# First token list from six half batches instead of eight, and the late half batches' logits in one matmul group each

## The chip, the cores and the metric

The kernel runs on one core of one Trainium2 chip. Its time is the device time of that core in microseconds, from launch to end. A profiled execution of the same program gives the trace that is read below. In it PE is the matrix engine, DVE the vector engine, ACT the scalar engine, POOL GpSimd and SP the engine that issues most DMAs; L56 is the line of a helper through which nearly all PE, DVE and ACT instructions pass, so groups are told apart by the names of their tiles.

## The reference, cut to what matters

A causal 7-tap filter per head runs along each sequence (8 sequences of 3584 tokens, 192 features, 8 heads of 24), with softmaxed taps; its output is routed over 8 experts with a capacity of 3584 tokens each, highest logits first, and every token passes the two-layer ReLU network of its expert.

```python
x_unf = x_pad[:, idx, :].reshape(B, S, K, H, group)
out = np.einsum('hk,bskhg->bshg', w, x_unf)          # w = softmax(weight) over the 7 taps
...
logits = x @ w_gate                                  # x: (28672, 192), w_gate: (192, 8)
order = np.argsort(-logits.flatten())
for idx in order:
    tok, e = (int(idx) // E, int(idx) % E)
    if assigned[tok] >= 0 or counts[e] >= cap:
        continue
    assigned[tok] = e
    counts[e] += 1
...
for e in range(E):
    mask = assigned == e
    h = np.maximum(x[mask] @ w1[e], 0.0)             # 192 -> 1024
    out[mask] = h @ w2[e]                            # 1024 -> 192
```

## The kernel before, in words

**Filter stage.** The tokens come in 16 half batches of 1792. `conv` (L196) loads one as 118 rows by 16 windows by 192 features, multiplies it for each of the 8 heads with a banded 118x128 matrix (PE `cv<-X,TH`, two records in the trace for one matmul), copies the sums out on ACT (`a<-cv`) and stores them to `attn` in DRAM. `transp` (L208) turns the result in 32x32 blocks on DVE (`aT<-a`, four per half batch). `logits` (L217) multiplies it with the gate weights: 24 matmuls for a half batch (six chunks of features, four column tiles of 32 columns, `pl<-aT,c_mu`), and `end` (L1560) transposes the sums (`pt<-ident,L`) into the table `LT` and takes each token's largest logit (`top`, L317). `LT` is 128 partitions by 8 experts by 256 columns; a half batch fills 16 columns. `gate(i, u)` (L1573) issues a third of the 24 matmuls. Since the conv matmuls of the next half batches run in between, `mid(h)` (L1603), called after the matmul of head h, puts the four transposes of half batch i-1 and, between them, the three gate groups and the end of half batch i-2 into the list `left`, and pops one entry (two, once the first list is done). From half batch LAG = 13 on, it pops nothing until the first list is done (`got`).

**Routing in the background.** The routing is one chain of Python generators, `Steps` (L75), with the parts `half(0)`, `tail`, `half(1)` and `rest`. While the program is written, `hook` runs a step of it when three modelled clocks (PE, DVE, ACT, class `Meter`) say that its inputs will be there and that DVE is not too far ahead; a step may ask to wait (`yield PEW`, a time, or `"cols", n` for n columns of `LT`). All of this is settled at build time; on the chip each engine executes its instructions in the order written, and waits on semaphores only.

A threshold `Ts` is found first (`thresh`, L322; its last part wants 96 columns). Tokens whose largest logit reaches it are settled at once on their best expert. A list of them is built from a set of columns of `LT` in these steps: `settle` marks them in `F`; `count` sums them per column (`bg<-ones,F`); `place` gives each its slot (`bg<-F,U`, `bg<-U,tot`, `bg<-ones,tot` for an offset of earlier columns); `slots` splits the slot numbers; `sort` brings the columns into slot order with one matmul per column (`bg<-X,oa`, 16 wide) from one-hot tiles `oa` made on DVE, and `turn` transposes the result on PE (`bg<-identb,X`); `sort4` does the same with 32-column tiles (`bg<-oa,X`), and turns it by a trip through DRAM on SP's queue (`otab<-X`, then `X<-otab`); `columns` makes the one-hot `c_oh`; `gather` adds up the list in PSUM (`bg<-iq,ones`, then 16 matmuls `bg<-c_oh,X`); `tokens` turns it into row numbers (`ia`, `ja`) on DVE. After `sort4`, `gather` is held back in the model by `there`, 10 us after the last copy.

- `half(0)`: threshold, then columns 0 to 127 (eight half batches), with `sort` and `turn`. It gives the first 512 tokens of each expert.
- `tail`: logits of half batches 14 and 15, which run in the first expert tile.
- `half(1)`: columns 128 to 255, with `sort4`, and `counts` and `open` ahead of its gather. It gives up to 2048 tokens of each expert.
- `rest`: seven rounds that settle the other tokens (`rounds`, L743), a last choice (`final`, L863), and a list of 1536 tokens per expert by two `sort4` and two `gather`, then `tokens` into `ib`, `jb`.

**Expert stage.** `FFN.run` (L1424) goes over 56 tiles of 512 tokens: tiles 0 to 7 are the first 512 tokens of the experts, tiles 8 to 31 the next 1536, tiles 32 to 55 the rest. For each tile and each of f = 0 to 7 it writes the first layer's five matmuls of chunk f (`ph`), then eight matmuls of the second layer of the tile before (`y`), with background steps at four points. Numbers are kept in two parts (`hh`, `hl`), hence the DVE work on each chunk. Rows of `attn` are gathered two tiles ahead on POOL (`xg<-attn,ja`). Ahead of that, at f = 0 of tile i, the row numbers of tile i+2 are asked for, and what of the background is then missing is written out at once:

```python
if t < 4:
    if len(bg.gens) > 1:
        bg.drain(1)
    return [(ja if rows else ia)[:, e, 4 * t + b:4 * t + b + 1] for b in range(4)]
if bg.gens:
    bg.drain()
```

Tiles 8 to 31 pass their inputs through DRAM on SP's queue (`turn` of `FFN`, L1388: `scr<-xs`, then `xs<-scr`), at f = 6, two tiles ahead. If a list is too short or an expert too full, a flag `bad` sends the program through a general path after the end; one of its conditions is that the first list has less than 512 tokens of an expert (`counts`, L657).

Of the kernel before, what the change touches and what calls it, by code (L numbers as in the profile page):

```python
# [259 lines left out]
class Route:  # L260
# [15 lines left out]
    def consts(self):  # L276
# [12 lines left out]
        self.g1 = cst.tile([128, 2], F32, name="g1")  # L289
        for h in range(2):  # L290
            P.tensor_scalar(self.g1[:, h:h + 1], pf, 1.0 + 128 * h, None, op0=OP.add)
# [81 lines left out]
    def settle(self, h):  # L373

        V, wk = self.nc.vector, self.wk
        s = slice(128 * h, 128 * h + 128)
        yield "cols", 128 * h + 128
        if h == 0:
            self.F = wk.tile([128, 8, G], BF, name="F")
        m = wk.tile([128, 128], F32, name="m_f")  # L380
        V.scalar_tensor_tensor(m, self.M1[:, s], self.Ts, self.M1[:, s], op0=OP.is_lt, op1=OP.add)
        for q in range(2):
            e = slice(4 * q, 4 * q + 4)
            V.tensor_tensor(self.F[:, e, s], self.LT[:, e, s], m[:, None, :].to_broadcast([128, 4, 128]),
                            op=OP.is_equal)
            yield PEW if q else None


    def count(self, F, h):
        nc, wk = self.nc, self.wk  # L390
        V, PE = nc.vector, nc.tensor
        s = slice(128 * h, 128 * h + 128)
        if h == 0:
            self.tot = [None, None]
            self.sl = wk.tile([128, G], F32, name="sl")
        ps = self.bg()
        for e in range(8):
            PE.matmul(ps[:, e:e + 1], F[:, e, s], self.ones[:, 0:1], start=True, stop=True, skip_group_check=True)
        t = self.tot[h] = wk.tile([128, 8], BF, name="tot%d" % h)
        nc.scalar.activation(t, ps[:, 0:8], AF.Copy)  # L400
        yield PEA

    def place(self, F, h, base):
# [3 lines left out]
        s = slice(128 * h, 128 * h + 128)  # L407
        SP = wk.tile([128, 8, 128], F32, name="X0")
        for q in range(2):
            ps = self.bg()  # L410
            f = F[:, 4 * q:4 * q + 4, s]
            PE.matmul(ps, self.U, f, start=True, stop=False, skip_group_check=True)
            for u in range(4):
                e = 4 * q + u
                o = ps[:, 128 * u:128 * u + 128]
                b = lambda t: t[:, e:e + 1].to_broadcast([128, 128])
# [1289 lines left out]
```

## Time and profile before

| | us |
|---|---|
| median of 3 runs | 1246.0 |
| lowest and highest run | 1242.64, 1251.04 |
| the profiled execution's own time | 1251.99 |
| span of its trace, first to last instruction | 1250.2 |
| PE busy | 1208.1 |
| DVE busy | 979.4 |
| ACT busy | 547.4 |
| POOL busy | 531.7 |
| DMA | 205.09 MB, 164 GB/s over the span |

The span is read by stages: the filter stage ends with the last `cv` at about 161 us of the trace, and the 56 tiles of the expert stage fill the rest. In the rows, the first column is the start in us from the span's start, the second the time until the end of the merged rows; matmuls overlap, so that what a group costs is read from its start to the start of what follows. `[1.53 <-DMA ...]` is idle time ahead of the row and what ended it.

### The profile page before, as it was taken

What the parts mean: (1) busy time and instruction counts of PE and PEld (TensorE: products, weight loads), DVE (VectorE), ACT (ScalarE), POOL (GpSimd) and SP (SyncE); (2) the same over time, 40 slices, a digit from 0 to 9 for tenths busy, and PEclk for the clock granted to TensorE, in tenths of its full rate; (3) what the DMA queues carried; (4) which work ended last, traced back from release to release, by engine and by line L of the source; (5) the groups of instructions that cost most, each with busy time, mean ns of one, the idle gap of its engine ahead of it and who ended that gap; (6) DMA issues with size and microseconds to landing.
All of it is one profiled execution on the core that took longest, in us unless ns stands there. A gap on an engine that the chain in (4) does not pass through costs nothing.

```text
span 1250.2 us, 21752 instructions
## 1 busy us (share of the span) xinstructions
PE 1208.1 (97%) x7702; PEld 1036.5 (83%) x7702; DVE 979.4 (78%) x2131; ACT 547.4 (44%) x1220; POOL 531.7 (43%) x528
## 2 busy tenths in 40 slices
PE   4999989999999999999999989999999999999997
PEld 2445568889988989889888879999999999999996
DVE  7388669889898898989888865777777777777772
ACT  4454555656444544444543333333443333443331
POOL 3000344535455545555454434445444544444522
PEclk9999999999999999999999999999999999999999
DMA  9999889999725463444344563114133222413100
GB/s 221 339 348 310 294 299 316 280 321 302 270 82 155 128 188 113 158 149 149 123 144 135 178 164 121 36 48 154 67 126 107 95 97 96 157 56 137 49 23 28
DMA packets 125188, 205.09 MB, mean 164 GB/s; under 512 B 21440, under 2 KB 85392, under 8 KB 121360
## 3 DMA queue, kind: packets, MB, share of 16 engines
q1 hardware_dynamic: 82464, 127.22, 31.9%
q0 software_dynamic: 21504, 44.07, 11.7%
q10 hardware_dynamic: 21104, 32.34, 7.8%
q8 instruction: 62, 1.02, 0.3%
q14 instruction: 54, 0.44, 0.1%
HBM read 118.64 MB, written 84.93 MB: 163 GB/s over the span
## 4 chain that ended last, share of the span: by engine, by line
PE 85%; DVE 6%; DMA 5%; issue 1%; SPq 1%; ACT 1%; POOL 1%; ACTq 0%; POOLq 0%; DVEq 0%
PE ph L56 40%; PE y L56 38%; PE bg L56 3%; PE cv L56 3%; DMA X<-in_x_dram 2%; DVE X L56 1%; DVE aT L56 1%; DMA wgr<-in_moe_w_gate_dram 1%; DMA raw<-in_moe_w_dram 1%; DMA X<-otab 1%; PE pl L56 1%; DMA xg<-attn,ja 1%; DVE hl L56 0%; PE px L56 0%; DMA otab<-X 0%
## 5 line engine op out<-in xcount | busy, mean ns | idle before, releaser
L56 PE MATMUL y<-w,hh 128*128 128x384 f32 x1792 | 536.8, 355 | 0.0
L56 ACT ACTIVATE hh<-ph 128x512 fp32r<-128x512 f32 x448 | 267.2, 597 | 486.3 <-PE ph L56 485.2
L56 PE MATMUL y<-w,hl 128*128 128x192 f32 x1792 | 449.7, 251 | 0.0
L56 DVE SCALAR_TENSOR_TENSOR hl<-ph,hh 128x512 fp32r<-128x512 f32 x448 | 308.5, 689 | 138.6 <-ACT hh L56 134.0
L56 PE MATMUL ph<-xa,w 128*128 128x512 f32 x1344 | 395.6, 402 | 0.0
L56 PEld LDWEIGHTS y<-w,hl 128*128 128x128 f32 x1792 | 341.7, 191 | 16.4
L56 PEld LDWEIGHTS y<-w,hh 128*128 128x128 f32 x1792 | 337.1, 188 | 20.4 <-issue 2.2
L56 PEld LDWEIGHTS ph<-xa,w 128*128 128x128 f32 x1344 | 218.9, 189 | 20.2 <-issue 1.0
L1348 POOL DMA_INDIRECT out_dram<-yo,ia x128 | 138.9, 1085 | 225.9 <-DVE yo L56 188.1
L1348 POOL DMA_INDIRECT out_dram<-yo,ib x96 | 95.9, 999 | 220.1 <-DVE yo L56 212.7
L56 PE MATMUL ph<-xd,w 128*128 128x512 f32 x448 | 178.9, 399 | 1.3 <-DVE xd L56 1.3
L56 PE MATMUL ph<-xd,dl 128*128 128x512 f32 x448 | 174.6, 390 | 0.2 <-DVE dl L56 0.2
L56 DVE STREAM_TRANSPOSE xs<-xg 32x128 f32<-32x128 f32 (+2 forms) x408 | 164.8, 404 | 6.6
L1273 POOL DMA_INDIRECT xg<-attn,ja x128 | 139.3, 1088 | 47.6 <-issue 40.4
L56 PE MATMUL cv<-X,TH 118*128 118x384 f32 x256 | 101.5, 523 | 19.5 <-DVE TH L56 12.5
L1273 POOL DMA_INDIRECT xg<-attn,jb x96 | 103.4, 1078 | 29.3 <-issue 29.3
L56 ACT ACTIVATE yt<-y 128x192 f32<-128x192 f32 x224 | 73.1, 326 | 94.3 <-PE y L56 92.3
L56 DVE TENSOR_TENSOR yo<-y,yt 128x192 f32<-128x192 f32 x224 | 79.5, 355 | 41.3 <-ACT yt L56 39.2
L56 PEld LDWEIGHTS ph<-xd,w 128*128 128x128 f32 x448 | 84.3, 188 | 21.4 <-DVE xd L56 1.7
L56 PEld LDWEIGHTS ph<-xd,dl 128*128 128x128 f32 x448 | 84.5, 189 | 19.7 <-issue 0.5
L56 PEld LDWEIGHTS cv<-X,TH 118*128 118x128 f32 x256 | 45.3, 198 | 49.9 <-issue 14.1
L56 ACT ACTIVATE a<-cv 128x384 f32<-128x384 f32 x128 | 59.5, 492 | 50.8 <-PE cv L56 33.0
(238 smaller groups left out, 893.1 us busy)
## 6 DMA issues: line engine op xcount, KB each, us to landing
attn<-a ACTq DMA_DIRECT2D x16, 1344.0 KB
w<-kw SPq DMA_DIRECT2D x14, 1536.0 KB
w<-kv SPq DMA_DIRECT2D x14, 1536.0 KB
kw<-w SPq DMA_DIRECT2D x48, 256.0 KB
kv<-w SPq DMA_DIRECT2D x32, 384.0 KB
X<-in_x_dram SPq DMA_DIRECT2D x17, 672.0 KB
X<-in_x_dram ACTq DMA_DIRECT2D x15, 672.0 KB
scr<-xs SPq DMA_DIRECT2D x96, 96.0 KB
```

Source lines behind the costliest of these rows:

```text
L56: return f(*a, **k)
L1273: self.nc.gpsimd.indirect_dma_start(out=t[:, b], out_offset=None, in_=self.attn[0:rows], in_offset=bass.IndirectOffsetOnAxis(ap=idx[b], ax ...
L1348: st = self.nc.gpsimd.indirect_dma_start(out=self.out, out_offset=bass.IndirectOffsetOnAxis(ap=idx, axis=0), in_=o, in_offset=None, bounds ...
```

## The change

`settle`, `count`, `place`, `columns`, `slots`, `sort`, `turn` and `gather` no longer take a half h of 128 columns but a part (first column, columns), and cut their tiles to its width. The first list is made of part (0, 96), six half batches. What was `half(1)` becomes `second`: columns 96 to 223 go through `sort4` as before; while its turn through DRAM is under way, the last part (224, 32) is settled and counted and the sums of `counts` are taken; then the first of the two is gathered, and the part of 32 columns is placed, sorted with `sort` (32 matmuls), turned on PE and gathered; `tokens` and `open` follow. The final lists of `rest` keep two halves of 128. In `mid`, half batches 11, 12 and 13 (from LAG = 13 on) get their 24 gate matmuls in one group, ahead of the transposes of the half batch behind them.

```diff
+PARTS = ((0, 96), (96, 128), (224, 32))
+HALVES = ((0, 128), (128, 128))
...
-    def place(self, F, h, base):
+    def place(self, F, part, bases):
...
-                if base is not None:
-                    PE.matmul(o, b(self.tot[base]), self.ones, start=False, stop=False, skip_group_check=True)
-                PE.matmul(o, b(self.tot[h]), self.U, start=False, stop=(u == 3), skip_group_check=True)
+                for p in bases:
+                    m = p[1]
+                    PE.matmul(o, self.tot[p][:, e:e + 1].to_broadcast([m, 128]), self.ones[0:m, 0:n],
+                              start=False, stop=False, skip_group_check=True)
+                PE.matmul(o, self.tot[part][:, e:e + 1].to_broadcast([n, 128]), self.U[0:n, 0:n],
+                          start=False, stop=(u == 3), skip_group_check=True)
...
-    def sort(self, h, nt, base, per=8):
+    def sort(self, part, nt, bases, per=8):
...
-        while z < 128:
+        while z < n:
...
-                if z == 64:
-                    yield from self.columns(h, nt, base)
+                if z == n // 64 * 32:
+                    yield from self.columns(part, nt, bases)
...
-    def lists(self, F, nt, h, base, idx, row, *part, between=None, swap=False):
+    def listed(self, F, nt, part, bases, between=None):
+
+        yield from self.place(F, part, bases)
+        yield from self.slots(F, part, between is None)
         if between is None:
-            yield from self.sort(h, nt, base)
-            yield from self.turn()
+            yield from self.sort(part, nt, bases)
+            yield from self.turn(part[1])
         else:
-            yield from self.sort4(h, nt, base)
+            yield from self.sort4(part, nt, bases)
             yield from between
-        yield from self.gather(nt, base is None)
-        yield from self.tokens(nt, idx, row, *part, swap=swap)
+        yield from self.gather(part[1], nt, not bases)
...
-        def half(h):
-            if h == 0:
-                yield from r.thresh(0.905)
-            yield from r.settle(h)
-            yield from r.count(r.F, h)
-            if h:
-                yield from r.counts(NE)
-            yield from r.lists(r.F, TA, h, 0 if h else None, *((ia, ja) if h else (ia0, ja0, 8, 4)),
-                               between=r.open() if h else None, swap=h == 1)
+        def early():
+            yield from r.thresh(0.905)
+            yield from r.settle(PARTS[0])
+            yield from r.count(r.F, PARTS[0])
+            yield from r.listed(r.F, TA, PARTS[0], ())
+            yield from r.tokens(TA, ia0, ja0, 8, 4)
+
+        def second():
+            yield from r.settle(PARTS[1])
+            yield from r.count(r.F, PARTS[1])
+            yield from r.listed(r.F, TA, PARTS[1], PARTS[0:1], between=third())
+            yield from r.listed(r.F, TA, PARTS[2], PARTS[0:2])
+            yield from r.tokens(TA, ia, ja, swap=True)
+            yield from r.open()
+
+        def third():
+            yield from r.settle(PARTS[2])
+            yield from r.count(r.F, PARTS[2])
+            yield from r.counts(NE)
...
-        bg = Steps(nc, r, (half(0), tail(), half(1), rest()))
+        bg = Steps(nc, r, (early(), tail(), second(), rest()))
...
+        def gates(i):
+            for u in range(3):
+                gate(i, u)
...
                 if i and h == 0:
+                    if i >= LAG:
+                        left.append(partial(gates, i - 2))
                     for u in range(4):
                         left.append(partial(k.transp, i - 1, u))
-                        if i > 1:
+                        if 1 < i and (u == 3 or i < LAG):
                             left.append(partial(gate, i - 2, u) if u < 3 else partial(end, i - 2))
```

Three places show how the instructions move. The first is on PE at the end of the filter stage, from the gather of the first list on, up to the end of half batch 12's logits; `cv` is the conv matmul of a head, `pl` the gate matmuls, `pt` the transpose of the sums. Before:

```order
L56 MATMUL cv<-X,TH 128x384 x4
L56 MATMUL pl<-aT,c_mu 32x128 x8
L56 MATMUL cv<-X,TH 128x384
L56 MATMUL pl<-aT,c_mu 32x128 x8
L56 MATMUL cv<-X,TH 128x384
L56 MATMUL pl<-aT,c_mu 32x128 x8
L56 MATMUL cv<-X,TH 128x384
L56 MATMUL pt<-ident,L 128x128
L56 MATMUL cv<-X,TH 128x384
L56 MATMUL pl<-aT,c_mu 32x128 x8
```

After:

```order
L56 MATMUL cv<-X,TH 128x384 x4
L56 MATMUL pl<-aT,c_mu 32x128 x24
L56 MATMUL cv<-X,TH 128x384 x2
L56 MATMUL pt<-ident,L 128x128
L56 MATMUL cv<-X,TH 128x384
L56 MATMUL pl<-aT,c_mu 32x128 x24
L56 MATMUL cv<-X,TH 128x384 x2
L56 MATMUL pt<-ident,L 128x128
```

The three groups of eight, with a conv matmul between them, are one group of 24. The gather ahead of these rows follows head 0 of half batch 14 before and head 2 of half batch 13 after, so the same half batch's logits also stand some heads earlier.

The second is on PE in the expert stage, at the last gather of the last list. `X_...` is a slab of the sort (`bg<-oa,X`) and, under another number, the turned list (`bg<-c_oh,X`); `y` is the second layer, `ph` the first. Before, these rows stand in f = 4 of tile 29, while the sort's last matmul stands in f = 7 of tile 28:

```order
L56 MATMUL y<-w_7888,hh 128x384
L56 MATMUL y<-w_7888,hl 128x192
L56 MATMUL y<-w_7888,hh 128x384
L56 MATMUL y<-w_7888,hl 128x192
L56 MATMUL ph<-xa,w_8385 128x512 x3
L56 LDWEIGHTS ones
L56 MATMUL bg<-iq,ones 128x192
L56 LDWEIGHTS X_9383
L56 MATMUL bg<-c_oh,X_9383 128x24
```

After, from the sort's last matmul on, in f = 7 of tile 29 and f = 0 of tile 30:

```order
L56 MATMUL bg<-oa,X_9233 32x128
L56 MATMUL y<-w_7978,hh 128x384
L56 MATMUL y<-w_7978,hl 128x192
L56 MATMUL y<-w_7978,hh 128x384
L56 MATMUL y<-w_7978,hl 128x192
L56 MATMUL y<-w_7978,hh 128x384
L56 MATMUL y<-w_7978,hl 128x192
L56 MATMUL y<-w_7978,hh 128x384
L56 MATMUL y<-w_7978,hl 128x192
L56 LDWEIGHTS ones
L56 MATMUL bg<-iq,ones 128x192
L56 LDWEIGHTS X_9699
```

The whole background has moved back by one tile by then, and the row numbers for tile 32 are asked for at f = 0 of tile 30, so the rest is written out there: eight `y` matmuls stand between the sort's last matmul and the gather, where before there were those eight, four whole steps of both layers and three `ph`.

The third is SP's queue at the same place; `scr` is the DRAM buffer of the tiles' inputs, `otab` that of the list, `kw` and `kd` are kept weights. Before:

```order
L546 DMA otab_81<-X_9012 128x2048
L1396 DMA scr_99<-xs 32x6x128 x4
L1398 DMA xs<-scr_99 128x512
L1399 DMA xs<-scr_99 64x512
L546 DMA otab_82<-X_9013 128x2048
L563 DMA X_9383<-otab_81 16x16x128 x4
L563 DMA X_9383<-otab_82 16x16x128 x4
L1231 DMA w_9436<-kw_84 128x3072
```

After:

```order
L557 DMA otab_81<-X_9325 128x2048
L1409 DMA scr_100<-xs 32x6x128 x4
L1411 DMA xs<-scr_100 128x512
L1412 DMA xs<-scr_100 64x512
L557 DMA otab_82<-X_9326 128x2048
L574 DMA X_9699<-otab_81 16x16x128 x4
L574 DMA X_9699<-otab_82 16x16x128 x4
L1251 DMA w_9793<-kv_102 128x3072
```

In both, the second half of the list (`otab_82`) is written behind the pass of a tile's inputs through `scr`, and read back at once. A load of weights (`kw_84`) that stood behind the list now stands ahead of its first half.

More of the change, by code (lines that the diff above doesn't have):

```diff
@@ L430, in columns @@
         nc, wk = self.nc, self.wk
         V, PE = nc.vector, nc.tensor
-        ps = self.bg()
-        PE.matmul(ps[:, 0:8], self.U, self.tot[h], start=True, stop=base is None)
-        if base is not None:
-            PE.matmul(ps[:, 0:8], self.ones, self.tot[base], start=False, stop=True)
-        bi = wk.tile([128, 2, 8], I32, name="c_bi")
+        c0, n = part
+        ps = self.bg()[0:n]
+        PE.matmul(ps[:, 0:8], self.U[0:n, 0:n], self.tot[part], start=True, stop=not bases)
+        for p in bases:
+            PE.matmul(ps[:, 0:8], self.ones[0:p[1], 0:n], self.tot[p], start=False, stop=p == bases[-1])
@@ L875, in final @@
             yield PEW if h else None
[L876 to L877 removed]
+        for p in HALVES:
+            yield from self.count(self.F, p)
         c = wk.tile([128, 3], F32, name="u_c")
```

138 lines of the change are left out of this document (72 added, 66 removed).

## The prediction

> **What bounds the kernel now.** I read the page's busy times and its chain of waits, then the table of busy time by stretches, PE's waits, and the order of time on PE at the two places that the change touches.
>
> ```profile
> PE 1208.1 (97%) x7702; PEld 1036.5 (83%) x7702; DVE 979.4 (78%) x2131; ACT 547.4 (44%) x1220; POOL 531.7 (43%) x528
> PE 85%; DVE 6%; DMA 5%; issue 1%; SPq 1%; ACT 1%; POOL 1%; ACTq 0%; POOLq 0%; DVEq 0%
> ```
>
> PE is busy 97% of the span and is 85% of the chain: what is put on it counts nearly one for one, and so does time in which it stands. Where it stands, at the end of the filter stage, the table by stretches shows (the stretch, its length, then busy time of PE, weight load, DVE, ACT and POOL, granted clock, DMA share, GB/s):
>
> ```profile
> 130.00:140.00 10.00, 10.00 (x98) 7.55 (x97) 2.36 (x4) 6.30 (x12) 0.00 (x0) 1.00 0.76 239
> 140.00:150.00 10.00, 9.23 (x83) 4.49 (x81) 9.21 (x23) 6.70 (x17) 6.25 (x6) 1.00 0.88 281
> 150.00:160.00 10.00, 8.35 (x98) 4.05 (x96) 5.28 (x8) 3.42 (x9) 8.44 (x9) 1.00 0.73 249
> 160.00:170.00 10.00, 8.69 (x105) 5.64 (x107) 8.84 (x14) 4.97 (x14) 4.97 (x5) 1.00 0.89 292
> ```
>
> PE is full to 140 us and then stands for 0.77, 1.65 and 1.31 us, 3.7 together. PE's waits (total us, times, longest) name what it stood for:
>
> ```profile
> PE pl L56 <- DVE aT L56: 1.9, 4, 0.8
> PE bg L56 <- DMA X<-otab: 3.3, 1, 3.3
> PE bg L56 <- DMA raw<-in_moe_w_dram: 1.6, 1, 1.6
> PE bg L56 <- DMA xg<-attn,ja: 1.5, 1, 1.5
> PE ph L56 <- DVE xd L56: 1.3, 1, 1.3
> PE bg L56 <- DVE F L56: 1.7, 2, 1.3
> ```
>
> The features still to be turned (`aT`), the first tile's rows (`xg`) and their second half (`xd`) make up those 3.7; the trip of a list through DRAM (`otab`) is a wait in the expert stage, for the last list; the wait put down to `raw` I take for the same trip of the second list, beside loads of weights. All are waits at the end of a list's making, and the change moves these ends.
>
> **The filter stage.** Prices first, from the order of time on PE (start, length, instruction, records merged, idle before):
>
> ```profile
> 114.98 1.65 PE L56 MATMUL bg<-X,oa 128*128 128x16 bf16 x24
> 116.49 1.54 PE L56 MATMUL cv<-X,TH 118*128 118x384 f32 x4
> ...
> 136.05 1.16 PE L56 MATMUL bg<-identb,X 128*128 128x128 bf16 x16
> 137.04 2.15 PE L56 MATMUL cv<-X,TH 118*128 118x384 f32 x6
> ...
> 139.04 0.27 PE L56 MATMUL bg<-iq,ones 128*128 128x256 bf16 x1
> ...
> 139.55 2.83 PE L56 MATMUL cv<-X,TH 118*128 118x384 f32 x8
> ...
> 142.31 0.64 PE L56 MATMUL pl<-aT,c_mu 128*32 128x128 f32 x16
> 142.88 0.91 PE L56 MATMUL cv<-X,TH 118*128 118x384 f32 x2
> 143.72 0.64 PE L56 MATMUL pl<-aT,c_mu 128*32 128x128 f32 x16
> ...
> 164.07 1.08 PE L56 MATMUL bg<-aT,c_mu 128*32 128x128 f32 x32
> 165.09 0.97 PE L56 MATMUL ph<-xa,w 128*128 128x512 f32 x3
> ```
>
> A sort matmul costs (116.49 - 114.98) / 24 = 0.063 us. The first list has 32 of them less: -2.0 us here. Its turn is still 16 matmuls (0.99) and its gather 17 (0.51); its shorter `place` saves about a tenth, which I leave out.
>
> A gate group and the conv matmul behind it take 143.72 - 142.31 = 1.41 us, with both changes of tile shape. Two groups in one piece take 1.02 against 0.57 for one, so a further group in the piece costs 0.45. A conv matmul not next to a group is 0.67 (three from 137.04 to 139.04). Three groups apart are 3 x 1.41 = 4.23; in one piece 1.41 + 2 x 0.45 + 2 x 0.67 = 3.65. That is -0.58 per half batch, and 11, 12 and 13 are treated so: -1.7 us. Half batches 14 and 15 keep their groups.
>
> Then the idle time. The rows of the first tile come after the list:
>
> ```profile
> 141.65 1.29 POOL L1254 TENSOR_TENSOR w<-raw,w 128x512 fp32r<-128x512 f32 x1 [32.54 <-ACT w L56]
> ...
> 146.34 1.25 POOL L1273 DMA_INDIRECT xg<-attn,ja  x1 [1.50 <-issue]
> ```
>
> ```profile
> 150.51 7.91 DMA xg<-attn,ja
> ```
>
> ```profile
> 158.46 0.33 PE L56 MATMUL bg<-ident,xg 128*128 128x128 f32 x1 [1.53 <-DMA xg<-attn,ja]
> ```
>
> From the gather at 139.04 to the landing of the first tile's fourth block (150.51 + 7.91 = 158.4) it is 19.4 us. In the changed order the gather stands at head 2 of half batch 13, and the transposes of those rows behind head 2 of half batch 15: 16 conv matmuls (10.7), three gate pieces (0.57 + 0.90 and about 0.2 for the two changes of shape, 5.0), the gather and three small transposes (0.9), 16.6 us later. The two subtractions of weights on POOL from 141.65, some 2.5 us, stood ahead of these gathers and now stand behind them; so the rows come about when they are wanted, with a wait between 0 and 2.8 us. The weights wait behind eight gathers instead, 8 x 1.25 us and the pauses between them; the first `ph` stands 21 conv matmuls and the rest, some 21 us, behind the list's gather, and that cover just holds. The `xd` wait goes: both halves are now transposed two heads before the stage ends. One wait is new: half batch 12's gates stand seven conv matmuls and one gate piece after the list, while its four turns on DVE are queued behind the list's last step; about 1 us. Of the 3.7 us I leave 1.3, a gain of 2.4, with 0 and 4.8 as the two ends of what stays. The earlier start of the list itself, with 96 columns ready instead of 128, costs nothing and brings nothing but this.
>
> Filter stage: -2.0 - 1.7 - 2.4 = -6.1 us, between -7.4 and -2.6.
>
> **The expert stage: a third part.** The 32 columns taken from the first list are now placed, sorted, turned and gathered among the tiles, where PE has no slack. `place` at full width:
>
> ```profile
> 196.73 0.22 PE L56 MATMUL bg<-ones,tot 128*128 128x128 bf16 x1
> ...
> 197.12 0.22 PE L56 MATMUL bg<-U,tot 128*128 128x128 bf16 x1
> ```
>
> Seven steps of 0.39 us: 0.056 each. The part of 32 columns has 24 such and two `bg<-F,U`: 1.5. Sort 32 x 0.063 = 2.0, turn 0.99, gather 0.51, and 13 tiny matmuls for `count`, `counts` and `columns` at about 0.04, 0.5. Sum +5.5 us. I take the full-width price for narrow matmuls, since each has a load of 128 weight columns as before. The Trainium skill (TensorEngine Tiling (Array Packing), Instruction Overhead) has it that a matmul carries about 60 cycles of overhead and one of free dimension 1 is as slow as one of 60; at the 2.4 GHz of TensorE: Matmul & The Clock Gate that is 25 ns, an estimate by which `place` and sort would be 2.0 us cheaper together. No row here has a matmul that fast with its own weights, so 0.056 and 0.063 stay.
>
> The work that DVE and ACT get for this lies beside the tiles and shows as delay of the background, except where PE waits for a step of DVE. Such a wait before `count` is in the trace (`DVE F`, 1.7 us over two lists); the third part has the same, so +1 us, between -0.5 and +3.
>
> **The last gather.** This is the largest term. The third part pushes the background back by a tile, and the gather meets the end of its time:
>
> ```profile
> 730.21 1.19 PE L56 MATMUL bg<-oa,X 128*32 128x128 bf16 x32
> 731.33 0.44 PE L56 MATMUL y<-w,hh 128*128 128x384 f32 x1
> ...
> 732.55 0.88 PE L56 MATMUL ph<-xa,w 128*128 128x512 f32 x3
> ...
> 742.42 0.26 PE L56 MATMUL bg<-iq,ones 128*128 128x192 bf16 x1
> 746.00 0.58 PE L56 MATMUL bg<-c_oh,X 128*128 128x24 bf16 x16 [3.32 <-DMA X<-otab]
> ```
>
> ```profile
> 732.02 3.01 DMA scr<-xs
> ...
> 736.00 4.36 DMA otab<-X
> ...
> 741.73 4.08 DMA X<-otab
> ```
>
> In these rows of PE, the sort's last matmuls end at 731.33, 1.2 us of `y` follow, and from 732.55 to 742.42 PE does four more steps and part of a fifth, 9.87 us. Then the gather stands 3.32 us until the list is back: SP is held by `scr`, writes `otab` from 736.00 for 4.36 us, reads it back until 741.73 + 4.08 = 745.8. In the changed order only the `y` stand between. SP's queue at that place is the same, so the list is back as late after the sort, and the 9.87 us of matmuls come after the wait instead of during it. PE stands about 13.2 us in place of 3.3: +9.9. If SP's hold by `scr` were gone, the write could start up to 3.5 us sooner: +6.4. If DMAs of the weights, moved ahead of it, slow the trip by half a DMA: +12. What follows is covered: before, DVE had the row numbers ready 5.8 us behind the gather, and the tile that they are for begins two tiles on, 16 steps of 2.3 us (9.87 us were 4.3 of them).
>
> ```profile
> 751.56 0.21 DVE L56 TENSOR_SCALAR jb<-m_y 128x96 int32<-128x96 f32 x1
> ```
>
> The clock falls in the wait before already (same columns as above, eighth is the clock):
>
> ```profile
> 746.00:748.00 2.00, 2.00 (x21) 1.81 (x22) 1.35 (x6) 0.34 (x1) 0.00 (x0) 0.50 0.97 412
> 752.00:754.00 2.00, 2.00 (x13) 1.80 (x12) 1.05 (x2) 0.72 (x2) 0.09 (x1) 1.00 0.00 0
> ```
>
> That half-speed stretch is paid already, about 5.3 us at half; a longer wait has the same one: 0, between -1 and +1.
>
> **Sum.** -6.1 + 5.5 + 1.0 + 9.9 = +10.3 us. Against the profiled execution's own 1251.99 that is 1262; that execution lies 6 us above the median of the runs shown, so for the median 1246.0 + 10.3 = 1256.
>
> **The rivals.** First, **the early start does not carry** (slower by more than 1%). The tiles 0 and 1 split their weights as these arrive, with DMA at 0.89 of its engines in the last row of the first table. If the weights or the first rows hold the first tile, PE starts as late as before whatever the list does, once rows or weights land more than about 4 us after the last conv matmul. Of the 6.1 us about 1 stays, in the half batches ahead of that point: the sum +15, 1261. For it: `raw` and `xg` stand among the waits. Against it: these loads are issued earlier too, and DMA has room between 130 and 160 us.
>
> Second, **the list returns sooner**: its write is not held by `scr`, and with PE standing and little else on the DMA engines each way is half a microsecond shorter. Then the stall is 13.2 - 3.5 - 1 = 8.7, the sum +5.8, 1252. By the Trainium skill (DMA: Bandwidth & Descriptors, Anatomy of one DMA) a transfer takes 2.0 us and its bytes at 436 GB/s; an estimate for 512 KB and 64 KB is 3.2 and 2.2 us, against 4.36 and 4.08 here, so the measured rows stand in the sum.
>
> Third, **not slower at all**: all of the filter stage's 3.7 us goes, and the whole trip is short: -7.4 + 5.5 - 0.5 + 6.4 - 1 = +3; to be faster it needs a further gain that no row shows. Fourth, **it does not do what it says**: were the first list under 512 tokens of an expert, the general path would run and add far more than the kernel's time. Six half batches hold 1344 tokens per expert on average and the threshold aims the fullest at 90.5% of capacity, so I give it 1 in 100.
>
> **How the numbers follow.** Changes under 1% (12.5 us) can't be told from none in a measurement of this kernel. My forecast has 0.57: its middle is +10.3 and its terms' ends spread it over +4 to +17, so a third of it lies above 12.5. The first rival has 0.2, all above; the second 0.17, all below; the third 0.05, of which 0.03 faster. Slower: 0.19 + 0.2 + 0.01 = 0.40; faster 0.03; same 0.57. The range leaves out 1 in 10 at each end: below, part of the third rival and of the second, +2; above, part of the first, +20: 1248 to 1266.
>
> **What would show it.** The sort of the first list with 96 matmuls, three gate pieces of 48 records, no `xd` wait, and the first `ph` 4 to 6 us earlier than 161, with nothing waited for behind it. A wait of PE for `otab` of 13 us in one piece near 750 us, with `bg<-c_oh,X` behind it, and half the clock after it. PE busy up by some 2 us only (+5.5 - 3.7). I am wrong if the first `ph` is not earlier, if that wait is under 8 us, or if other waits of PE in tiles 2 to 9 sum to over 3 us more.

## The result and the profile after

The changed kernel takes 1264.1 us, the median of four runs (1259.2 to 1265.4), beside 1247.8 for the kernel before on the same chip: a ratio of 1.0124, 95% interval 1.0089 to 1.0159. By that ratio it is +15.5 us (+11.1 to +19.8; the medians differ by 16.3), slower by about 1.2%. The time lies in the range of 1248 to 1266, near its upper end and above the forecast of 1256. The profiled execution took 1262.95 us, span 1261.1; against the 1251.99 of the one before that is +11.0.

The page's busy times:

```profile
PE 1215.1 (96%) x7774; PEld 1044.5 (83%) x7774; DVE 977.3 (77%) x2153; ACT 548.6 (44%) x1223; POOL 527.9 (42%) x530
```

PE is busy 7.0 us more, where the prediction had about 2. The table by stretches, cut at the same instructions in both traces, shows where it went. The cuts are: the first conv matmul of half batch 9, the first `ph`, and the first `ph` of tiles 2, 9, 25 and 31. Columns: the stretch, its length, then busy time of PE, weight load, DVE, ACT and POOL, granted clock, DMA share, GB/s. The kernel before:

```profile
0.00:90.03 90.03, 69.09 (x492) 36.08 (x493) 58.08 (x153) 42.51 (x107) 13.23 (x46) 0.98 1.04 300
90.03:161.16 71.13, 67.19 (x647) 39.55 (x645) 53.38 (x103) 36.19 (x91) 16.14 (x17) 1.00 0.93 294
161.16:200.71 39.55, 36.66 (x294) 29.46 (x292) 31.83 (x64) 21.54 (x48) 14.45 (x14) 1.00 0.97 341
200.71:341.55 140.84, 139.20 (x921) 124.73 (x920) 127.49 (x276) 79.58 (x171) 65.46 (x58) 1.00 0.90 293
341.55:644.11 302.56, 301.69 (x1730) 270.26 (x1729) 267.91 (x611) 139.02 (x344) 159.84 (x145) 1.00 0.46 140
644.11:775.57 131.46, 127.67 (x967) 112.20 (x966) 94.54 (x190) 52.31 (x107) 59.94 (x56) 0.97 0.50 150
```

and the changed one:

```profile
0.00:86.85 86.85, 68.69 (x492) 35.73 (x492) 57.90 (x153) 41.99 (x107) 13.12 (x48) 0.98 1.04 310
86.85:151.26 64.41, 63.23 (x615) 39.97 (x613) 48.35 (x101) 35.66 (x90) 15.71 (x17) 1.00 0.95 301
151.26:194.20 42.94, 38.11 (x287) 29.61 (x285) 31.84 (x56) 21.27 (x48) 12.73 (x13) 0.96 0.98 338
194.20:346.79 152.59, 150.36 (x1028) 133.02 (x1027) 125.24 (x280) 80.23 (x171) 67.39 (x57) 0.98 0.84 273
346.79:647.26 300.47, 300.47 (x1726) 269.97 (x1724) 265.34 (x610) 139.63 (x344) 157.75 (x147) 1.00 0.47 142
647.26:786.69 139.43, 127.61 (x976) 112.03 (x975) 102.42 (x220) 53.52 (x111) 59.61 (x55) 0.96 0.48 141
```

| stretch | length | of it PE busy | idle |
|---|---|---|---|
| start to half batch 9 | -3.18 | -0.40 | -2.78 |
| half batch 9 to the first tile | -6.72 | -3.96 | -2.76 |
| tiles 0 and 1 | +3.39 | +1.45 | +1.94 |
| tiles 2 to 8 | +11.75 | +11.16 | +0.59 |
| tiles 9 to 24 | -2.09 | -1.22 | -0.87 |
| tiles 25 to 30 | +7.97 | -0.06 | +8.03 |
| tiles 31 to the end | -0.2 | 0.0 | -0.2 |

The first row is mostly waiting for the first loads, ahead of all that the change touches; without it the profiles differ by 14.1 us, within the interval of the timed runs. PE's waits (total us, times, longest) give names to the rest:

```profile
PE bg L56 <- DMA X<-otab: 11.6, 1, 11.6
PE ph L56 <- DVE hl L56: 3.2, 4, 2.3
...
PE bg L56 <- DMA kw<-w: 1.7, 1, 1.7
```

The wait for `otab` grew from 3.3 to 11.6; the one for `hl` is new; the one put down to `kw<-w` stands at the second list's gather, where 1.6 us were put down to `raw` before. The order of time on PE at the three places:

```profile
168.41 0.99 PE L56 MATMUL ph<-xa,w 128*128 128x512 f32 x3 [2.30 <-DVE hl L56]
...
240.44 0.28 PE L56 MATMUL bg<-iq,ones 128*128 128x256 bf16 x1
242.47 0.55 PE L56 MATMUL bg<-c_oh,X 128*128 128x32 bf16 x16 [1.75 <-DMA kw<-w]
242.87 0.22 PE L56 MATMUL bg<-F,U 128*128 128x128 bf16 x1
242.93 0.20 PE L56 MATMUL bg<-ones,tot 96*128 96x32 bf16 x2
...
752.31 1.20 PE L56 MATMUL bg<-oa,X 128*32 128x128 bf16 x32
...
754.66 0.26 PE L56 MATMUL bg<-iq,ones 128*128 128x192 bf16 x1
766.54 0.58 PE L56 MATMUL bg<-c_oh,X 128*128 128x24 bf16 x16 [11.62 <-DMA X<-otab]
```

Behind the second of them the clock falls (stretches of 2 us, columns as above, the eighth is the clock):

```profile
242.00:244.00 2.00, 1.53 (x30) 1.32 (x31) 0.42 (x1) 0.00 (x0) 1.49 (x2) 1.00 1.06 373
244.00:246.00 2.00, 2.00 (x17) 1.72 (x17) 0.94 (x3) 0.52 (x1) 0.54 (x1) 0.58 0.98 309
```

The trace's record of the granted clock has it at half from 244.3 for 6.83 us, with PE full all the time: 3.4 of the 11.16 us by which PE is busier in tiles 2 to 8.

### The profile page after: what moved, and what is told of

Read it like the earlier page. It is cut to its first block, busy times and chain, and to the rows that moved or that the text cites. A ratio compares the mean times of both kernels' runs of the same rounds, so it can differ in the third digit from the quotient of the medians.

```text
span 1261.1 us, 21921 instructions
## 1 busy us (share of the span) xinstructions
PE 1215.1 (96%) x7774; PEld 1044.5 (83%) x7774; DVE 977.3 (77%) x2153; ACT 548.6 (44%) x1223; POOL 527.9 (42%) x530
## 4 chain that ended last, share of the span: by engine, by line
PE 87%; DMA 6%; DVE 4%; ACT 1%; SPq 1%; POOL 1%; issue 1%; POOLq 0%; ACTq 0%; DVEq 0%
PE ph L56 40%; PE y L56 39%; PE bg L56 3%; PE cv L56 3%; DMA raw<-in_moe_w_dram 2%; DMA X<-in_x_dram 1%; DVE aT L56 1%; DVE X L56 1%; DMA wgr<-in_moe_w_gate_dram 1%; PE pl L56 1%; DMA attn<-a 1%; PE px L56 0%; DMA otab<-X 0%; ACT a L56 0%; DVE hl L56 0%
## 5 line engine op out<-in xcount | busy, mean ns | idle before, releaser
L56 PEld LDWEIGHTS y<-w,hl 128*128 128x128 f32 x1792 | 341.9, 191 | 16.3
```

What stands on the lines that cost most here:

```text
L56: return f(*a, **k)
```

## The experiments

Each kernel is read at its stage by the same cuts as above, since single terms of 1 to 5 us are near or under what timing resolves; ratios are to the kernel before, run on the same chip beside it. On the chip of four of the kernels (named there) the kernel before took 1257.1 us, and all of those waited 2 to 4 us more in stages that no edit touches.

### The merged gate groups alone

The kernel before, with `mid` of the changed one:

```diff
+                    if i >= LAG:
+                        left.append(partial(gates, i - 2))
                     for u in range(4):
                         left.append(partial(k.transp, i - 1, u))
-                        if i > 1:
+                        if 1 < i and (u == 3 or i < LAG):
```

> The kernel before, with the gate matmuls of half batches 11, 12 and 13 merged into one group of 24 each, and nothing else of the change. Theory (the prediction's term): three times 0.58 us less in the filter stage; from half batch 10 to the first `ph` it takes 61 us where before it took 62.8; the whole time is 1.7 us less, a ratio to before of 0.9986, too little for the comparison, so the stage decides. Rival: the 7.15 us that this stage lost in the changed kernel come from the shorter list alone, and a group of 24 brings nothing, since the four transposes on DVE behind it come later by as much: 62.8 us again, ratio 1.000.

Measured: 1246.1 us, ratio 0.9971 (0.9956 to 0.9985). Half batch 10 to the first tile, in the kernel before and in this one:

```profile
98.38:161.16 62.78, 59.18 (x581) 35.43 (x579) 45.64 (x85) 31.89 (x80) 15.89 (x16) 1.00 0.92 286
```

```profile
97.16:158.63 61.47, 58.59 (x580) 37.38 (x579) 46.62 (x86) 31.81 (x81) 15.78 (x16) 0.97 0.91 288
```

The stage is 1.3 us shorter, with one stretch at half clock in it that the kernel before did not have. PE is busy 0.6 us less there, and 1.9 less in the last experiment below, which has the same groups and no such stretch (57.27 against 59.18). The term of -1.7 fits that; more than its sign and size to a microsecond these traces do not give, as the stage differs by about as much from one profile to the next (60.55 us in that last experiment).

In the profiles, one of each kernel, the rest came from where nothing was edited, tiles 25 to 30: 128.40 us, 3.1 less than before. PE's order of time and the clock at the last gather:

```profile
742.54 0.55 PE L56 MATMUL bg<-c_oh,X 128*128 128x24 bf16 x16 [2.71 <-DMA X<-otab]
```

```profile
740.00:744.00 4.00, 1.46 (x22) 1.41 (x23) 1.01 (x6) 0.32 (x1) 1.40 (x2) 1.00 1.07 310
744.00:748.00 4.00, 4.00 (x24) 3.62 (x23) 3.83 (x14) 1.21 (x3) 0.00 (x0) 1.00 0.52 189
```

A wait of 2.71 us and no half clock behind it; before, 3.32 us and 6.8 us at half. The last section comes back to this.

### What holds tiles 0 and 1

The list ends earlier, and the first `ph` stands at 151.26 and not 161.16. Taking off the 3.2 us that both traces already differ by at half batch 9, that is 6.7 us, and 3.4 of them are lost in the next two tiles. Two theories: the queue order that the prediction had named, with the subtractions on POOL ahead of SP's loads, and the DMA engines.

```diff
                 if i >= 14 and h % 2:
-                    ff.wsplit(-1, P)
+                    ff.wsplit(-1, V)
```

> The changed kernel, with the subtractions of the first weights (four of them, written during half batches 14 and 15) on DVE and not on POOL. Theory: on POOL they stand behind the eight gathers of the first rows until 146.74 us; SP's stores of the split weights wait for them, and the loads of the next weights wait behind these stores. On DVE the loads go out some 5 us sooner, the waits of PE for `hl` in tile 0 and 1 (2.30 and 0.42 us) go, and with them the half-speed stretch at 169.2 us: tiles 0 and 1 take 39.6 us where the changed kernel has 42.9; 3.4 us less in all, 1260.7, ratio to before 1.010. Rival: the DMA engines are full then (gathers, stores of `attn`, loads), the weights land no sooner however soon they are asked for: tiles 0 and 1 take 42 to 43 us, time 1264, ratio 1.013.

Measured: 1261.9 us, ratio 1.0100 (1.0077 to 1.0123). Tiles 0 and 1, PE's waits there, and SP's next load of weights in the changed kernel and in this one:

```profile
151.43:194.75 43.32, 38.13 (x287) 30.43 (x285) 31.75 (x56) 21.35 (x48) 12.59 (x13) 0.96 0.96 329
PE ph L56 <- DVE hl L56: 2.5, 1, 2.5
```

```profile
148.44 2.14 SPq L1227 DMA_DIRECT2D raw<-in_moe_w_dram  x1
```

```profile
142.87 0.56 SPq L1227 DMA_DIRECT2D raw<-in_moe_w_dram  x1
```

This load goes out 5.6 us sooner and the next three 1.9 to 6.6 us sooner, and the tiles take 43.3 us as before the edit. So the theory of the subtractions on POOL falls: they held these loads, but not the time. The fifth load went out no sooner (160.58 us, 160.06 in the changed kernel): a store of split weights (`kv<-w`) stands ahead of it on SP's queue in both. (The time was 2 us under the changed kernel's, most of it in tiles 2 to 8, where PE waited 1.15 us less; that was not looked into.) Then the stores of expert 0's split weights were left out; later tiles of that expert load those of expert 1, so that the output differs:

```diff
+        if e == 0:
+            pass
-        if what == "w":
+        elif what == "w":
             S.dma_start(self.kept2[e][:, s], t[4][:, s].bitcast(F32))
```

and the loads of `kept1`, `keptd` and `kept2` take `e or 1`.

> The changed kernel without the stores of expert 0's split weights to DRAM (3.4 MB; when its weights are wanted again, those of expert 1 are loaded, so the values of later tiles are others while every instruction is the same). Theory after the run with the subtractions on DVE: the DMA engines are full from 155 to 180 us (shares of 0.96 to 1.04), the loads of the weights come as fast as the bytes ahead of them go, and the list that ended earlier finds them not there. With 3.4 MB less, at some 310 GB/s, the wait of PE for `hl` (2.30 us) and the half-speed stretch behind it go, tiles 0 and 1 take 39 to 40.5 us where the changed kernel has 42.9. Rival: ACT, which stands for the issue of the last `attn` store until 156.4 us and splits the weights in between the first `hh`, sets the pace, whatever the loads do: tiles 0 and 1 take 42.5 us or more.

Measured on the slower chip, so by tiles 0 and 1 alone; the second row is another kernel of the same batch with the copies in (the write on ACT's queue, below):

```profile
154.39:192.13 37.74, 36.37 (x286) 29.27 (x285) 32.05 (x56) 21.59 (x48) 13.11 (x12) 1.00 0.90 305
```

```profile
153.79:199.76 45.97, 38.67 (x287) 30.99 (x285) 30.93 (x55) 21.45 (x48) 11.51 (x12) 0.93 0.93 313
```

37.7 us against 42.7 to 46.0 in the changed kernels with the copies, and the clock stays whole. So, by these single profiles, the copies hold these tiles. Whether by their bytes is not shown: without them the loads behind them on SP's queue go out sooner as well. The fifth stands 5.6 us behind the first `ph` (160.03 - 154.39), where the changed kernel has 8.8 (160.06 - 151.26), and the sixth 7.0 where it has 13.3. No run took away the bytes and left the queue as it was. The same edit in the kernel before:

> The kernel before without the stores of expert 0's split weights (3.4 MB; later tiles of expert 0 load those of expert 1, every instruction is the same), as in the same edit of the changed kernel, where tiles 0 and 1 took 37.7 us. Theory: before, the list ended so late that the weights were there; the 39.56 us of tiles 0 and 1 hold 1.31 us of waiting for `xd` and 1.58 for `F`, no wait for weights, and stay 38.5 to 40. Rival: the full DMA engines hold these tiles in the kernel before as well: they take 37.5 us or less.

```profile
158.75:197.04 38.29, 36.62 (x295) 29.43 (x292) 31.98 (x64) 21.59 (x48) 15.54 (x15) 1.00 0.91 305
```

38.3 us where it had 39.56, a little under the theory's 38.5 to 40 and over the rival's 37.5: PE waits 1.2 us less, as the wait for `F` is gone. In single profiles, and those of the changed kernel from two chips, the copies cost the changed kernel 5.2 us in these tiles and the one before 1.3.

### The part of 32 columns in tile 4

```diff
         def third():
             ...
             yield from r.counts(NE)
+            yield from r.place(r.F, PARTS[2], PARTS[0:2])
+            yield from r.slots(r.F, PARTS[2], True)
...
-            yield from r.listed(r.F, TA, PARTS[2], PARTS[0:2])
+            yield from r.sort(PARTS[2], TA, PARTS[0:2])
+            yield from r.turn(PARTS[2][1])
+            yield from r.gather(PARTS[2][1], TA, False)
```

> The changed kernel, with `place` and `slots` of the part of 32 columns written ahead of the second list's first gather, while that list is on its trip through DRAM, and not right behind it. Theory: tile 4 takes 31.6 us (21.6 before) because 1.75 us of waiting and 2.7 us of narrow matmuls right behind them leave PE nearly unused for 4.5 us, and the clock is halved for 6.8 us from 244.3; apart, the wait is covered and the clock stays: tiles 2 to 8 take 147.5 us where the changed kernel has 152.6; 5 us less in all, 1259, ratio to before 1.009. Rival: it is the work itself (107 more background records in these tiles), and no order of it helps: tiles 2 to 8 take 151 us or more, time 1262.5 or more, ratio 1.012.

Measured: 1259.9 us, ratio 1.0086 (1.0067 to 1.0104). Tiles 2 to 8:

```profile
195.90:342.59 146.69, 146.69 (x1028) 130.57 (x1027) 124.63 (x281) 80.30 (x171) 68.14 (x58) 1.00 0.87 284
```

5.9 us less with the same 1028 matmul records, no idle time and a full clock: the theory holds in this trace (the same order with two edits, below, lost the clock once more). What stays over the 139.20 us of PE work before is 7.5 us, the work of the third part. The narrow `place` in this trace, the start and the last of its 26 matmuls and what follows (each step has two `ones,tot`, with weights of 96 and of 128 rows, and one `U,tot` with weights of 32 rows):

```profile
240.37 0.23 PE L56 MATMUL bg<-F,U 128*128 128x128 bf16 x1
240.44 0.21 PE L56 MATMUL bg<-ones,tot 96*128 96x32 bf16 x2
240.58 0.18 PE L56 MATMUL bg<-U,tot 32*128 32x32 bf16 x1
240.70 0.21 PE L56 MATMUL bg<-ones,tot 96*128 96x32 bf16 x2
...
242.50 0.19 PE L56 MATMUL bg<-U,tot 32*128 32x32 bf16 x1
242.61 0.44 PE L56 MATMUL y<-w,hh 128*128 128x384 f32 x1
```

2.24 us for 26, 0.086 each in the mean, where matmuls of full width took 0.056. A step of three is 0.26 us (240.70 - 240.44); in the single records the 128-row matmul starts 0.03 us behind the 96-row one, the 32-row one 0.11 behind that, and the next step's 96-row one another 0.12.

### The last gather

The rows of tile 32 are asked for four steps later:

```diff
-                if i + 2 < n and f == 0:
+                if i + 2 < n and f == (4 if tiles[i + 2][1][1] > 3 and tiles[i + 1][1][1] < 4 else 0):
```

> The changed kernel, with the rows of tile 32 (the first that needs the last list) asked for at f = 4 of tile 30 and not at f = 0, so that the last gather may stand four steps later. Theory: the stall of 11.62 us is the list's trip through DRAM with its cover gone; four steps of 2.29 us are 9.2 us of cover: a stall of 2.4 us stays, a half-speed stretch of 3.4 to 6.8 us in place of 10.2, tiles 25 to 30 take 128 to 130 us where the changed kernel has 139.4; in all 10 to 11 us less, 1253.5, ratio to before 1.0045. Rival: what follows the gather becomes the wait (row numbers on DVE 3.5 us, four gathers on POOL 5.3 us and their landing, then the transposes of tile 32): PE waits near the start of tile 32, and the time falls by 3 us or less, 1261, ratio 1.0105.

Measured: 1255.3 us, ratio 1.0046 (1.0032 to 1.0060), as the theory had it. Tiles 25 to 30, a little over its 128 to 130 us, and the gather:

```profile
652.08:782.69 130.61, 127.78 (x977) 112.26 (x975) 102.42 (x220) 53.58 (x111) 55.98 (x52) 0.99 0.50 148
```

```profile
771.50 0.55 PE L56 MATMUL bg<-c_oh,X 128*128 128x24 bf16 x16 [2.61 <-DMA X<-otab]
```

The four steps are 9.2 us, the wait fell from 11.62 to 2.61, and nothing that follows the gather took its place. Then the trip itself, the prediction's second rival (on the slower chip):

```diff
-                    S.dma_start(self.otab[z // 2 - 1], O[z // 2 - 1])
+                    (S if z == 2 else A).dma_start(self.otab[z // 2 - 1], O[z // 2 - 1])
```

> The changed kernel, with the last write of a list to DRAM (`otab`, second half) issued on ACT's queue, right behind the copy that makes it, and not on SP's, where it stands behind the write and the reading back of `scr`. This is the prediction's second rival made by hand. Theory: of the stall of 11.62 us 3.5 are SP's hold (the copy ends at 754.15, the write is issued at 757.67): 8.1 us stay; 3.5 us less, and the clock as before or one half-speed stretch less: tiles 25 to 30 take 134 to 136 us where the changed kernel has 139.4. Rival: the reading back is on SP still, behind `scr`, and shares the DMA engines with it: the stall stays over 10.5 us and tiles 25 to 30 over 138.

SP's queue in the changed kernel, and SP's in this one:

```profile
752.75 1.80 SPq L1409 DMA_DIRECT2D scr<-xs  x4
756.73 0.34 SPq L1411 DMA_DIRECT2D xs<-scr  x1
...
757.67 0.54 SPq L557 DMA_DIRECT2D otab<-X  x1
758.29 5.33 SPq L574 DMA_DIRECT2D X<-otab  x8
```

```profile
763.42 1.80 SPq L1409 DMA_DIRECT2D scr<-xs  x4
768.58 0.34 SPq L1411 DMA_DIRECT2D xs<-scr  x1
...
769.51 3.97 SPq L574 DMA_DIRECT2D X<-otab  x8
```

The gather's wait is 11.53 us, 11.2 in the other changed kernel on that chip. The write left SP's queue, but the eight loads of `X<-otab` stand on it still, behind `xs<-scr`, which waits for `scr` to land. Tiles 25 to 30 take 141.8 us: the theory falls, and its rival holds. Whether the trip is shorter with the loads off that queue too was not tried.

### Sums, and what the old lists give

Three edits together (late rows, early `place`, the write on ACT's queue), on the slower chip:

> The changed kernel with three edits at once: rows of tile 32 asked for four steps later, the part of 32 columns placed while the second list is on its trip, and the lists' last write on ACT's queue. Theory (the losses lie apart and add up): tiles 2 to 8 146.7 us, tiles 25 to 30 128 us, no stall at the last gather and no half-speed stretch there; 5.9 and 11 us less than the changed kernel, 1247, ratio to before 0.999 (0.995 to 1.002): the change then costs nothing and brings nothing. Rival: one of the waits comes back in another place (rows of tile 32 late, the second gather's wait), ratio 1.004 or more.

Measured: 1258.5 us beside 1257.1 for the kernel before, ratio 1.0013 (0.9995 to 1.0030). Tiles 2 to 8 took 146.71 us, tiles 25 to 30 132.84; the wait at the last gather is 2.6 us. The losses add up, but for that wait. The old lists with the merged groups and the write on ACT's queue, on the same chip:

> The kernel before (lists of 128 and 128 columns), with the merged gate groups and the lists' last write on ACT's queue. Theory: the stall at the last gather (2.7 us in the run with merged groups alone) goes, as the write starts 3.5 us sooner: 1243.5, ratio to before 0.9955, and faster than any kernel with a third part, whose 5.5 us of PE work are not in it. Rival: with the stall under 3 us the trip is covered anyway and the write on ACT holds up ACT's copies: ratio 0.997 or more, as with the merged groups alone.

Measured: 1257.9 us, ratio 0.9999 (0.9985 to 1.0014); the gather still waits 2.5 us. The rival holds here too, but for its ratio: the 0.3% of the merged groups alone are not seen on this chip, and whether the write on ACT took them or the chip did is open.

Then the two ways side by side. The changed kernel with late rows and early `place`:

> The changed kernel with the rows of tile 32 asked for four steps later and the part of 32 columns placed during the second list's trip. Theory: 8.8 and 5.9 us less than the changed kernel, as each brought alone, so 14.7 of its 16: ratio to before 1.000 (0.997 to 1.003), and above that of the old lists with the later gather run beside it by 0.005, since 7 us of PE work of the part of 32 columns stay and 6 us of the filter stage are gone, 3.4 of them given back in tiles 0 and 1. Rival: with both gone the shorter filter stage shows: ratio 0.996 or less, no slower than the old lists with the later gather.

and the old lists with merged groups and later gathers:

```diff
-            yield self.there
+            yield self.there + (0.0 if first else 4.0)
```

> The kernel before (lists of 128 and 128 columns) with the merged gate groups, and the second list's gather and the last one held back 14 us after the last copy and not 10 us. Theory: the stall of some 3 us at the last gather and the 1.6 us at the second list's go, with them every half-speed stretch there: 1.3 us from the groups, 4.5 us from the waits, up to 2.5 us from the clock; ratio to before 0.9945 (0.992 to 0.997). Rival: what is later by two steps is waited for elsewhere (rows of tile 8 or 32): ratio 0.997 or more.

Measured: the changed kernel with two edits 1251.8 us, ratio 1.0025 (1.0009 to 1.0041). The old lists with the later gather 1242.05 us, ratio 0.9948 (0.9934 to 0.9962), the fastest kernel of all and better than both given ones. Its tiles 2 to 8 and 25 to 30:

```profile
196.97:337.06 140.09, 139.50 (x921) 124.61 (x919) 123.67 (x266) 78.11 (x168) 64.12 (x57) 1.00 0.90 294
```

```profile
639.94:765.64 125.70, 125.15 (x967) 110.27 (x966) 94.22 (x190) 52.36 (x107) 59.95 (x56) 1.00 0.52 157
```

PE is idle 0.6 us in each, and the trace has no stretch at half clock before the very end. Tiles 2 to 8 of the changed kernel with two edits, and two windows of the clock in tile 4:

```profile
198.39:346.80 148.41, 148.41 (x1029) 131.90 (x1027) 125.70 (x283) 80.31 (x171) 67.28 (x59) 0.99 0.85 281
```

```profile
242.43:245.85 3.42, 3.42 (x36) 2.87 (x35) 1.91 (x9) 0.60 (x1) 2.60 (x3) 1.00 0.80 175
245.85:249.26 3.41, 3.41 (x12) 2.95 (x12) 3.07 (x11) 1.76 (x4) 2.03 (x2) 0.50 1.02 322
```

PE is never idle here by its busy time, and still the clock falls for 3.41 us, behind a window in which 2.2 of 3.4 us are `place`: that is why these tiles take 1.7 us more than with the early `place` alone.

The two kernels differ by 9.8 us, their profiles by 11.6 from half batch 9 on. By the same cuts that is -4.5 us up to the first tile, +4.1 in tiles 0 and 1, +8.3 in tiles 2 to 8, -2.4 in tiles 9 to 24, +6.0 in tiles 25 to 30, where the changed kernel still waits 3.7 us at the last gather, and +0.1 behind. So what the shorter first list brings in front is gone two tiles later, and the third part's work stays.

## Why the prediction was right, and where its terms were off

The range held the time; the sign, and that the last gather is the largest wait, were right. With 1.24% the time lies over the 1% line, on the side that had a chance of 0.40; the interval (0.89 to 1.59%) reaches under the line, to the side that had 0.57. The sum of +10.3 was some 5 us short of the timed +15.5, and 3.8 short of the 14.1 that the profiles give from half batch 9 on. That it missed by no more is in part luck: tiles 0 and 1 gave back 3.4 us that no term had, and tiles 2 to 8 cost 5.3 us more than their terms (11.75 against 6.5), while tiles 25 to 30 cost 1.9 less than theirs and tiles 9 to 24, which had none, took 2.1 less. By its steps:

- **Filter stage, -6.1.** It came to -6.7, inside the ends. The idle time fell by 2.76 where the term had 2.4, and PE's work by 4.0 where sort and groups had 3.7. No wait for `xd`, gate pieces of 48 records, and the first `ph` 6.7 us earlier, counted from half batch 9, a little more than the 4 to 6 named.
- **"That cover just holds"** (the weights behind eight gathers). This step failed. The weights were late, PE waited 2.30 us for `hl`, lost the clock for 3.4 us, and gave back 3.4 us. The cause that the step named, the subtractions on POOL, was wrong too: moved to DVE they changed nothing, and without the 3.4 MB of copies it all came back (by their bytes, or by their places on SP's queue: open). The prediction had read "DMA has room between 130 and 160 us", a share of 0.73 to 0.89; but the loads for tiles 0 and 1 are moved from 155 us on, where the share is near 1. The first rival, which was to leave 1 of 6.1 us, was half right.
- **The third part, +5.5 and +1.0 of waits.** The work was 7.5 us: `place` cost 2.24 and not 1.5, as its rows show 0.11 to 0.12 us at each change to weights of 32 rows and back; the tiny matmuls and the turn cost the rest. The sort's 32 matmuls took 2.0, as priced. The estimate from the Trainium skill (TensorEngine Tiling (Array Packing), Instruction Overhead), by which `place` and sort were to be 2.0 us cheaper, lay on the wrong side for these two. But the reason given against it, that no row has a matmul so fast with its own weights, was a misreading: the 16 of the gather at 139.04 us, each with its own weight load in the trace, start 0.025 us apart. The waits were +0.6 us.
- **The clock, 0 ±1.** This term failed, and is the one that was most under size. It was read at the last gather alone, and there it holds: PE's busy time in tiles 25 to 30 is the same within 0.1 us, since the longer half-speed stretch lies in the wait. But 6.83 us at half clock came in tile 4 and 3.41 in tiles 0 and 1, 5.1 us of work together. The difference between PE's busy time forecast (+2) and found (+7.0) is about as large; in it the third part's further 2.0 us of work stand against less work in the filter stage and in tiles 9 to 24.
- **The last gather, +9.9.** The mechanism was right to the row: only the `y` stand between the sort and the gather, and the wait is in one piece. It was 11.62 us and not 13.2, as the list was back 13.1 us after the sort's end and not 14.7 (766.54 - 753.44 against 746.00 - 731.33): +8.3, within its ends. A further 0.9 us of idle time and 1.2 us of work went in tiles 9 to 24; why is open.
- **The second rival** (the list returns sooner if its write is not held) gave 3.5 us to SP's hold of the write. Made by hand it gave nothing. The 1 us that it gave to emptier DMA engines fits the trip, which was 1.6 us shorter; what shortened it no run tells. (The fit that it took from the Trainium skill (DMA: Bandwidth & Descriptors, Anatomy of one DMA) is stated there for DMAs issued by GpSimd, while the list's are issued by SP; it stands in no term.)

The timed difference of 15.5 us lies 1 to 5 us over those of the profiles (14.1 from half batch 9 on, 10.9 in all). The larger gap comes from which executions were profiled: the one of the kernel before took 1251.99 us, 4.2 over that kernel's median, the other 1262.95, 1.1 under its own.

## What to carry to other kernels

Work that ends earlier is worth only what its consumers can take: before an early start is counted, read the DMA share, and the queue, where the consumer's own loads are moved, not where the early work ran. Work moved to a later place must be priced with the slack of the next deadline behind it, here a whole tile of 18.3 us that had covered a trip through DRAM. Where such a wait is left, holding its consumer back by two steps of other work costs one number in the program: together with the merged groups it gave 0.5% here, and moved lists cost 1.2%.

## What the hardware showed that was not expected

**A wait costs its length and the phase of a window.** In the traces' records the clock changes only at steps of 3.413 us. Cut into windows on that grid and set against PE's idle time, the 13 profiles give, up to the last tile: 32 full-speed windows with 1.95 us or more of idle time, and all 32 are followed by a window at half clock; nearly 60 windows with 1.0 to 1.95 us, 8 of them followed by one. Those 8 include tile 4, where narrow matmuls fill the rest of the window (1.57 us idle in the changed kernel). So the same wait can be cheap or dear by where it falls: 3.32 us fell as 1.97 and 1.35 in the kernel before and cost 6.8 us at half clock; 2.71 us fell as 1.66 and 1.05 in the one with merged groups and cost none. The Trainium skill (TensorE: Matmul & The Clock Gate, Part 1: The HAM clock gate) has the window as free-running and 3413 ns long, which agrees; it has the clock fall after one idle window, and here some 2 us idle of the 3.4 were enough. No edit moved a wait against the grid on purpose, so that the phase decides is read from these traces, not tried.

**The clock can fall with PE busy.** Two more windows at half clock follow windows with under 1 us of idle time: 0.84 us, beside gate and sort matmuls (late rows, 109.8 us), and none, beside the 26 matmuls of `place` (two edits, above). With three edits the same 26 lay inside one window too, and the clock stayed. So PE's busy time, in which a matmul of `place` counts some 0.18 us though the next one starts after 0.03 to 0.12, is not all that decides; what else does, these traces do not tell.

**The rows of the weights set the price of `place`, not its columns.** The rows of `place` above have 0.03 us from a matmul with 96 rows to one with 128, and 0.11 to 0.12 us at each change to 32 rows and back. With 128 rows all along, the matmuls took 0.056 us at 128 columns (`place` at full width) and 0.025 us at 32 (the gather). No run changed the rows alone, so the reading rests on these rows.
